# Attention into a token and channel mixer on one core: second token weights through SyncE's queue, token layer a pass later, first channel weights in two transfers

## The chip, the cores and the metric

The kernel runs on one core of one Trainium2 chip. The metric is the device time of one execution in microseconds; before, the median of three runs is 382.45 us (380.16 to 384.23). The engines are TensorE (PE, its weight loads PEld), VectorE (DVE), ScalarE (ACT), GpSimd (POOL) and SyncE (SP). SP here does nothing but issue DMA transfers; POOL issues DMA transfers too, and a transfer that changes the type (FP32 in memory, FP16 on chip) is issued by POOL in this kernel.

## The reference

```python
# q, k, v: (8, 12, 448, 64); tau = 0.1
q_n = q / (norm(q) + 1e-6);  k_n = k / (norm(k) + 1e-6)
attn = softmax(q_n @ k_n.T / tau)
x = (attn @ v) -> (8, 448, 768)                # heads side by side
h = relu(x.T @ w_tok1) @ w_tok2                # token mixer: 448 -> 256 -> 448
u = x + h.T
out = u + relu(u @ w_ch1) @ w_ch2              # channel mixer: 768 -> 1536 -> 768
```

Inputs and output are FP32; on chip the products are in FP16 with FP32 sums.

## The kernel before

**Pairs and passes.** Two heads of one batch make a pair; 6 pairs (`NPAIR`) make a batch, 48 pairs the whole. The order of every engine's work is written out by hand (`tc.manual_schedule()`): a prologue for pair 0, then a loop whose pass `i` handles pair `i`. Passes 1 to 5 are one loop, pass 6 is written out on its own, and from pass 7 on a third loop runs. Names with a number in this document (q10, v8, tok2(0)) mean the pair.

**What a pass does.** Loads run ahead: `load_qk(i + 6)` and `load_v(i + 4)`, each a 224 KB transfer (for the first twelve pairs) on SyncE's queue. `square(i + 3)` squares k on POOL and, in passes 1 to 5, q on ACT; `sums(i + 2)` adds them up on DVE; `norms` makes the reciprocal norms on ACT and DVE; `scaled(i + 1)` scales k and q into FP16 on POOL; `tpose(i + 1)` transposes them on PE. `score(i, c)` for four chunks c is a PE product followed by an exponential on ACT (L350). `cast_v` makes v FP16 on POOL. `pv_wide(i - 1)` and `x_wide(i - 1)` give the attention output x of the pair before.

**The token mixer.** `tok1(i)` multiplies x(i) by the first token weights and takes the relu on DVE. `tok2(i)` multiplies by `w2t`, the second token weights in their chunk order, and adds x on DVE, which gives u (L441). In passes 2 to 5 `tok1(i - 2)` and `tok2(i - 2)` are done in the same pass.

**From tokens to channels.** The channel mixer needs u transposed (`ut`). For the first two pairs of batch 0 `udma` does it with a DMA transpose on SyncE's queue (L447), issued at the ends of passes 2 and 3. Pairs 2 and 5 are transposed on PE and copied by ACT (`upose_act`), pairs 3 and 4 on PE and copied by DVE (`upose`). From pass 7 on a queue of channel products (`m_ch1`: L471, `m_ch2`: L487) is drawn from between the attention products. The first of them, six matmuls over the six parts of `ut`, stands in pass 7; its first matmul reads what udma(0) wrote, its second what udma(1) wrote.

**The weights.** POOL's queue loads them all, with the change of type: the first token weights in eight small transfers (`weights_tok1`), `w2n` (`weights_tok2`, 224 KB, early in the prologue), the first channel weights `wc1t` in four transfers of 576 KB (L203; a half of the columns and a half of the rows each), issued in passes 2, 4, 5 and 6, and later the second channel weights `wc2t` in two of 1152 KB (L208). `place_w2` (L198, pass 2) copies `w2n` into `w2t` on POOL with the columns taken in steps of four. `w2n` borrows one of the three buffers of the output rows (`ost`), which are first needed much later.

**Queues.** SyncE issues in the program's order, and an issue waits where its buffer is not free yet or where the eighth transfer before it has not landed. POOL issues its transfers between its own computations, in the program's order. Both queues are served by the same 16 DMA engines.

Of the kernel before, what the change touches and what calls it, by code (L numbers as in the profile page):

```python
# [7 lines left out]
FP32 = mybir.dt.float32  # L8
FP16 = mybir.dt.float16
# [13 lines left out]
def kernel(  # L23
# [12 lines left out]
    nc = tc.nc  # L36

    B, H, S, E = q.shape
    D = H * E
    T = moe_w_tok1.shape[1]  # L40
    C = moe_w_ch1.shape[1]
    SC = 112
    NCH = S // SC
    DT = D // 128
    CT = C // 128
    TT = T // 128
# [23 lines left out]
    def windows(b):  # L70
        return EVEN if b % 2 == 0 else ODD

    def pieces(lo, hi):
        got = []
        while lo < hi:
            c = lo // SC
            end = min(hi, SC * (c + 1))
            got.append((c, lo - SC * c, end - SC * c))
            lo = end
        return got  # L80
# [4 lines left out]
    outp = ctx.enter_context(tc.tile_pool(name="outp", bufs=3))  # L85
# [13 lines left out]
    def old(i):  # L99
        return i < OLD  # L100
# [12 lines left out]
    def load_rows(i, nm, src, bufs):  # L113
        h0 = 2 * (i % NPAIR)
        if old(i):
            t = pool_of(nm).tile([SC, QS, E], FP32, name=f"{nm}f_{i}", tag=f"{nm}f", bufs=bufs)
            nc.sync.dma_start(
                out=t[:].rearrange("p (g c) e -> p g (c e)", g=2),
                in_=src[h0:h0 + 2].rearrange("g (p c) e -> p g (c e)", c=NCH))
            return t  # L120
        t = pool_of(nm).tile([128, 2 * KC, E], FP32, name=f"{nm}f_{i}", tag=f"{nm}f", bufs=bufs)
        nc.sync.dma_start(out=t[:].rearrange("p (g c) e -> p g (c e)", g=2),
                          in_=src[h0:h0 + 2, 0:128 * KC].rearrange("g (p c) e -> p g (c e)", c=KC))
        return t

    def load_rest(i, nm, src):
        h0 = 2 * (i % NPAIR)
        t = (att if nm == "v" else rest).tile([128, HP, E], FP32, name=f"{nm}r_{i}", tag=f"{nm}r", bufs=4)
        for g in range(2):
            nc.sync.dma_start(out=t[64 * g:64 * g + 64],  # L130
                              in_=src[h0 + g:h0 + 2 * HP:2, 128 * KC:S].rearrange("j p e -> p j e"))
        return t
# [13 lines left out]
    def load_v(i):  # L146
        pipe[i]["v"] = load_rows(i, "v", v[i // NPAIR], 4)
        if not old(i) and "vr" not in half[i // HP]:
            half[i // HP]["vr"] = load_rest(i, "v", v[i // NPAIR])
# [7 lines left out]
    nc.gpsimd.memset(tiny[:], 1e-18)  # L157

    w1t = cst.tile([128, 5, T], FP16, name="w1t")
    w2n = outp.tile([128, TT, S], FP16, name="w2n", tag="ost")  # L160
    w2t = cst.tile([128, TT, S + 64], FP16, name="w2t")
    wc1t = cst.tile([128, DT, C], FP16, name="wc1t")
    wc2t = cst.tile([128, CT, D], FP16, name="wc2t")
# [17 lines left out]
    def weights_tok1(n0, n1):  # L181
        todo = []
        for m, (lo, hi) in enumerate(MAIN):
            r = 0
            for c, p0, p1 in pieces(lo, hi):
                todo.append((p1 - p0, m, r, c, p0))
                r += p1 - p0
        (c, p0, p1), = pieces(384, S)
        todo = sorted(todo + [(64, 3, 0, c, p0)]) + [(64, 4, 64, c, p0)]
        for n, m, r, c, p0 in todo[n0:n1]:  # L190
            nc.gpsimd.dma_start(out=w1t[r:r + n, m, :],
                                in_=moe_w_tok1.rearrange("(p c) t -> c p t", c=NCH)[c, p0:p0 + n])

    def weights_tok2():
        nc.gpsimd.dma_start(out=w2n[:], in_=moe_w_tok2.rearrange("(tt p) s -> p tt s", p=128))

    def place_w2():
        nc.gpsimd.tensor_copy(out=w2t[:, :, 0:S].rearrange("p t (c s) -> p t c s", c=NCH),  # L198
                              in_=w2n[:].rearrange("p t (s c) -> p t c s", c=NCH))

    def weights_ch1(i):
        cols, t = slice(768 * (i // 2), 768 * (i // 2) + 768), 3 * (i % 2)
        nc.gpsimd.dma_start(out=wc1t[:, t:t + 3, cols],  # L203
                            in_=moe_w_ch1[128 * t:128 * t + 384, cols].rearrange("(t p) c -> p t c", p=128))

    def weights_ch2(i):
        cols = slice(DH * i, DH * (i + 1))
# [48 lines left out]
    def some(i, a0, a1):  # L256
        sl, np_ = lay(i)
        return max(np_[a0:a1]), slice(sl[a0].start, sl[a1 - 1].stop)
# [9 lines left out]
    def norms(i, a0=0, a1=2, dve=False, rec=None):  # L268
        rec = dve if rec is None else rec
        st = pipe[i]  # L270
        n, sl = some(i, a0, a1)
        rn = st["rn"][0:n, sl]
        ne = nes[i % 3][0:n, sl]
        if dve:
            nc.vector.tensor_reduce(out=rn, in_=ne, axis=AXX.X, op=ALU.add)
            if not rec:
                return
        if dve or rec:
            nc.vector.reciprocal(out=rn, in_=rn)  # L279
            return  # L280
        nc.scalar.activation(out=rn, in_=st["ssq"][0:n, sl], func=AF.Ln, bias=tiny[0:n])
        nc.scalar.activation(out=ne[:, :, 0], in_=rn, func=AF.Exp, scale=0.5)
# [30 lines left out]
    def scaled(i):  # L313
        scale(i, 0)
        scale(i, 1)
# [102 lines left out]
    def tok1(i, wide=False):  # L418
        st = pipe[i]
        w1 = (0, 1, 2, 3) if (i // NPAIR) % 2 == 0 else (4, 0, 1, 2)  # L420
        psR = (ps2 if wide else ps).tile([128, TT, 128], FP32, name=f"psR_{i}", tag="s" if wide else "b")
        for tt in range(TT):
            for m in range(4):
                nc.tensor.matmul(psR[:, tt], w1t[:, w1[m], tt * 128:(tt + 1) * 128], st["x"][:, m],  # L424
                                 start=(m == 0), stop=(m == 3))
        st["rt"] = nrm.tile([128, TT, 128], FP16, name=f"rt_{i}", tag="rt", bufs=2)
        nc.vector.tensor_scalar_max(out=st["rt"][:], in0=psR[:], scalar1=0.0)  # L427

    def tok2(i, pe=False, wide=False):
        st = pipe[i]  # L430
        b, pj = i // NPAIR, i % NPAIR
        if pj == 0:
            u16[b] = mix.tile([128, DT, 4, 128], FP16, name=f"u16_{b}", tag="u16", bufs=4)
            ut[b] = mix.tile([128, DT, 4, 128], FP16, name=f"ut_{b}", tag="ut")
        psU = (ps2 if wide else ps).tile([128, 4, 128], FP32, name=f"psU_{i}", tag="s" if wide else "b")
        for m, lo in enumerate(windows(b)):
            for tt in range(TT):
                nc.tensor.matmul(psU[:, m], w2t[:, tt, lo:lo + 128], st["rt"][:, tt],  # L438
                                 start=(tt == 0), stop=(tt == TT - 1))
        u = u16[b][:, pj]  # L440
        nc.vector.tensor_tensor(out=u, in0=psU[:], in1=st["x"][:], op=ALU.add)  # L441
        if not pe:
            udma(i)

    def udma(i):
        b, pj = i // NPAIR, i % NPAIR
        nc.sync.dma_start_transpose(out=ut[b][:, pj], in_=u16[b][:, pj].rearrange("p m d -> p (m d)"))  # L447
# [28 lines left out]
    ost = {}  # L476
# [299 lines left out]
    with tc.manual_schedule():  # L776
# [3 lines left out]
            name=nc.get_next_instruction_name(), act_func_set_id=ACT_SET_LN_EXP,  # L780
# [7 lines left out]
        load_v(2)  # L788
        load_qk(5)
        load_v(3)  # L790
        weights_tok1(0, 7)

        square(0, 1, act=True)
# [7 lines left out]
        norms(0, 0, 1, dve=True)  # L801
        scale_part(0, 0, 0, 2, nc.gpsimd)
        scale_part(0, 0, 2, NCH, nc.gpsimd)
        weights_tok2()
        square(1, 1, act=True)
        square(1, 0, act=True)
        square(2, 1, act=True)
# [35 lines left out]
        for i in range(1, NPAIR):  # L843
            if i == 1:
                scale(2, 0)
                scale(2, 1, nc.vector)
            else:
                scaled(i + 1)
                if i == 3:
                    weights_tok1(7, 8)  # L850
                else:
                    weights_ch1(max(i - 3, 0))
            load_qk(i + 6)
            score(i, 0)
            score(i, 1)
            sums(i + 2)
            norms(i + 2)
            if i >= 2:
                tok1(i - 2)
            pv_wide(i - 1)  # L860
            x_wide(i - 1)
            norms(i + 2, dve=True)
            cast_v(i)
            if i == 2:
                place_w2()
            square(i + 3, 0)
            if i == 1:
                warm(10)
            score(i, 2)
            score(i, 3)  # L870
            tpose(i + 1)
            if i >= 2:
                tok2(i - 2, pe=True)
            square(i + 3, 1, act=True)
            load_v(i + 4)
            if 2 <= i < 4:
                udma(i - 2)

        i = NPAIR
        load_qk(i + 6)  # L880
# [2 lines left out]
        score(i, 1)  # L883
        sums(i + 2)
        norms(i + 2)
        tok1(i - 2)
        pv_wide(i - 1)
        x_wide(i - 1)
# [7 lines left out]
        upose_act(i - 4, True)  # L896
        norms(i + 2, dve=True)
        scaled(i + 2)
        weights_ch1(3)
        tok1(i - 1)  # L900


# [216 lines left out]
```

## Time and profile before

| | us |
|---|---|
| median of three runs | 382.45 (380.16, 382.45, 384.23) |
| profiled execution | 381.04 |
| its span | 379.3 |
| PE busy in the span | 364.9 (96%) |
| POOL, DVE, ACT busy | 286.4, 246.3, 233.7 |
| PE idle in the first 10 us; from 10 to 40; from 40 to 340 | 3.6; 4.9; 0.5 |
| DMA moved | 64.35 MB, 170 GB/s over the span |

The profile's page counts an engine as busy while an instruction of it runs. PE's matmuls overlap, so its busy time is no measure of its rate, but a gap in it is a real gap. The rows that the next section shows are of four kinds: a table of stretches, the orders of time of single engines (start, duration, engine and line, what it writes and reads, and in brackets the idle time before it with what ended that), and, for one transfer, its issue (start) with the time from there to its landing.

### The profile page before, as it was taken

Reading aid. Unit: us, or ns where it says so; the run is one execution under the profiler, and the core shown is the slowest. Engines: PE = TensorE matmul, PEld = TensorE weight load, DVE = VectorE, ACT = ScalarE, POOL = GpSimd, SP = SyncE. Lnnn points to the kernel's source line nnn. Section 1 sums busy time; section 2 is a strip of 40 time slices with the busy share of each in tenths; the row PEclk is TensorE's granted clock in tenths of the full one; section 3 lists DMA queues with packets and bytes.
Section 4 is the critical chain, followed back from the end, with each engine's and each line's share of the span. In section 5 each row is a group of like instructions: output and inputs, shape, how many; then the busy total and the mean of one; then the engine's idle time right before and its main releaser. Section 6 shows DMA issues by size and latency. Waiting matters only on the chain.

```text
span 379.3 us, 10291 instructions
## 1 busy us (share of the span) xinstructions
PE 364.9 (96%) x4096; PEld 238.8 (63%) x4096; DVE 246.3 (65%) x560; ACT 233.7 (62%) x401; POOL 286.4 (76%) x414
## 2 busy tenths in 40 slices
PE   6789999999999999999999999999999999999994
PEld 5466666676657666667666666666666676655562
DVE  7788866776436674557544675466545776887963
ACT  5999887855665447855675466774677574526410
POOL 8899998978667577668657757767869987389760
PEclk9999999999999999999999999999999999999998
DMA  7999999989985888869895877997995874200144
GB/s 203 270 250 218 261 252 233 178 161 167 228 193 133 207 193 203 177 168 171 208 208 125 175 184 190 201 169 186 212 178 116 159 160 99 57 0 3 54 125 114
DMA packets 116256, 64.35 MB, mean 170 GB/s; under 512 B 72304, under 2 KB 112880, under 8 KB 116208
## 3 DMA queue, kind: packets, MB, share of 16 engines
q1 hardware_dynamic: 110208, 58.20, 69.0%
q0 software_dynamic: 5616, 5.21, 8.7%
q8 instruction: 32, 0.52, 0.6%
q10 hardware_dynamic: 384, 0.29, 0.2%
q14 instruction: 16, 0.13, 0.1%
HBM read 43.45 MB, written 11.01 MB: 144 GB/s over the span
## 4 chain that ended last, share of the span: by engine, by line
PE 84%; DMA 5%; DVE 4%; ACT 3%; POOL 2%; issue 0%; SPq 0%; DVEq 0%; POOLq 0%
PE psG L471 21%; PE psF L487 21%; PE psO L388 9%; PE psS L349 8%; PE psU L438 5%; PE psR L424 5%; DMA kf<-in_k_dram 4%; PE psY L591 3%; PE psYo L679 2%; ACT pt L350 2%; PE psX L591 2%; PE psQ L356 2%; PE psZ L591 1%; PE psO L371 1%; DMA qk<-kq 1%; PE psZo L679 1%
## 5 line engine op out<-in xcount | busy, mean ns | idle before, releaser
L350 ACT ACTIVATE pt<-psS 128x896 f16<-128x896 f32 (+1 forms) x156 | 132.7, 915 | 52.4 <-PE psS L349 52.4
L487 PE MATMUL psF<-wc2t,gt 128*128 128x384 f16 x504 | 88.4, 326 | 0.0
L471 PE MATMUL psG<-ut,wc1t 128*128 128x448 f16 x432 | 88.1, 352 | 0.0
L302 POOL TENSOR_TENSOR kq<-kf,rn 128x384 f16<-128x384 f32 (+1 forms) x47 | 41.8, 889 | 59.7 <-DVE rn L279 56.7
L487 PEld LDWEIGHTS <-gt 128*128 128x128 f16 x504 | 47.1, 98 | 27.8
L471 PEld LDWEIGHTS <-wc1t 128*128 128x128 f16 x432 | 40.2, 98 | 32.4
L474 ACT ACTIVATE gt<-psG 128x448 f16<-128x448 f32 x72 | 38.8, 539 | 33.2 <-PE psG L471 33.2
L266 DVE TENSOR_REDUCE ssq<-sq 128x15 f32<-128x960 f32 (+2 forms) x51 | 56.1, 1100 | 2.9 <-POOL kq L302 1.1
L427 DVE TENSOR_SCALAR rt<-psR 128x256 f16<-128x256 f32 x48 | 20.1, 418 | 50.8 <-PE psR L424 50.8
L302 POOL TENSOR_TENSOR kq<-qf,rn 112x512 f16<-112x512 f32 x45 | 46.9, 1043 | 3.0
L349 PE MATMUL psS<-qk 64*128 64x448 f16 x312 | 40.9, 353 | 3.5 <-DVE qk L328 2.6
L491 DVE TENSOR_TENSOR ost<-psF,u 128x384 f32<-128x384 f32 (+1 forms) x48 | 25.8, 537 | 26.8 <-PE psF L487 26.7
L250 POOL TENSOR_TENSOR sq<-kf 128x384 f32<-128x384 f32 (+1 forms) x46 | 40.1, 872 | 0.9 <-DMA kf<-in_k_dram 0.9
L250 POOL TENSOR_TENSOR sq<-qf 112x512 f32<-112x512 f32 x39 | 40.5, 1038 | 0.0
L388 PE MATMUL psO<-vt,pt 128*128 128x65 f16 (+1 forms) x1024 | 39.1, 193 | 0.0
L392 DVE TENSOR_TENSOR x<-psO,rec 128x256 f16<-128x256 f32 x82 | 34.8, 425 | 2.8
L388 PEld LDWEIGHTS <-pt 128*128 128x128 f16 (+1 forms) x1024 | 34.2, 97 | 3.5 <-issue 0.9
L441 DVE TENSOR_TENSOR u<-psU,x 128x512 f16<-128x512 f32 x48 | 32.4, 674 | 2.3 <-PE psU L438 0.9
L438 PE MATMUL psU<-rt,w2t 128*128 128x128 f16 x384 | 29.3, 219 | 0.9 <-POOL w2t L198 0.9
L438 PEld LDWEIGHTS <-w2t 128*128 128x128 f16 x384 | 24.8, 98 | 8.4 <-POOL w2t L198 1.1
L424 PEld LDWEIGHTS <-w1t 128*128 128x128 f16 x384 | 24.8, 98 | 7.9 <-issue 2.1
L424 PE MATMUL psR<-x,w1t 128*128 128x128 f16 x384 | 29.3, 219 | 0.2 <-DVE u L441 0.2
(128 smaller groups left out, 478.4 us busy)
## 6 DMA issues: line engine op xcount, KB each, us to landing
qf<-in_q_dram SPq DMA_DIRECT2D x47, 224.0 KB, 4.0
kf<-in_k_dram SPq DMA_DIRECT2D x36, 192.0 KB, 3.6
vf<-in_v_dram SPq DMA_DIRECT2D x36, 192.0 KB, 3.6
vf<-in_v_dram SPq DMA_DIRECT2D x12, 224.0 KB, 8.3
kf<-in_k_dram SPq DMA_DIRECT2D x11, 224.0 KB, 8.2
wc1t<-in_moe_w_ch_dram POOLq DMA_DIRECT2D x4, 576.0 KB, 10.0
wc2t<-in_moe_w_ch_dram POOLq DMA_DIRECT2D x2, 1152.0 KB, 12.2
out_dram<-ost SPq DMA_DIRECT2D x6, 336.0 KB, 4.4
```

The lines of the kernel that those rows point to most:

```text
L250: nc.gpsimd.tensor_mul(out=dst, in0=src, in1=src)
L266: nc.vector.tensor_reduce(out=st["ssq"][0:n, sl], in_=st["sq"][0:n, sl], axis=AXX.X, op=ALU.add)
L302: eng.tensor_tensor(out=kq[0:p, a, 0:n].rearrange("p c g e -> p g c e"), in0=st["kq"[a]][:].rearrange("p (g c) e -> p g c e", g=2), in1=_b ...
L349: nc.tensor.matmul(psS[:, hh, 0:S], qk[hb, c * n:c * n + 128], qm[hb], start=True, stop=True)
L350: nc.scalar.activation(out=pts[i % 2][0:n, 2 * S * c:2 * S * (c + 1)].rearrange("p (h s) -> p h s", h=2), in_=psS[0:n, :, 0:S], func=AF.Ex ...
L388: nc.tensor.matmul(psO[:, m, 0:E + 1], pts[i % 2][0:n, at:at + 128], vt[0:n, i % HP, nch * hh + c, 0:E + 1], start=(old(i) and c == 0), st ...
L392: nc.vector.tensor_tensor(out=st["x"][:, :, hh * E:(hh + 1) * E], in0=psO[:, :, 0:E], in1=_bcast_free(rec[:], E), op=ALU.mult)
L424: nc.tensor.matmul(psR[:, tt], w1t[:, w1[m], tt * 128:(tt + 1) * 128], st["x"][:, m], start=(m == 0), stop=(m == 3))
L438: nc.tensor.matmul(psU[:, m], w2t[:, tt, lo:lo + 128], st["rt"][:, tt], start=(tt == 0), stop=(tt == TT - 1))
L471: nc.tensor.matmul(psG[:, 0:S], wc1t[:, dt, ct * 128:(ct + 1) * 128], ut[b][:, dt].rearrange("p m s -> p (m s)")[:, lo:lo + S], start=(dt ...
L474: nc.scalar.activation(out=gt[:, ct, (b % 2) * S:(b % 2 + 1) * S], in_=psG[:, 0:S], func=AF.Relu)
L487: nc.tensor.matmul(psF[:, 0:hi - lo], gt[:, ct, at:at + 128], wc2t[:, ct, lo:hi], start=(ct == 0), stop=(ct == CT - 1))
```

## The change

1. `w2n` becomes two FP32 tiles of 128 x 768, of which 448 columns are used, in two of the three `ost` buffers. They are loaded by SyncE, one 224 KB transfer each, behind `load_v(3)` and so ahead of v4, q6, k6 and all later loads. POOL no longer issues a transfer for them.
2. `place_w2` becomes two POOL copies that also change the type, in pass 3 instead of pass 2.
3. `tok2` comes a pass later: tok2(0) in pass 3, tok2(1) in pass 4, tok2(2) in pass 5; pass 6 has tok2(3), at a place of its own ahead of `tok1(4)`, and tok2(4) where it was. From pass 7 on nothing is moved.
4. The two `udma` follow: udma(0) at the end of pass 3, udma(1) at the end of pass 4. In SyncE's queue udma(1) now stands behind q10, k10 and v8.
5. `wc1t` is loaded in two transfers of 1152 KB (all rows, a half of the columns), issued in passes 2 and 4, instead of four in passes 2, 4, 5 and 6.

```diff
-    w2n = outp.tile([128, TT, S], FP16, name="w2n", tag="ost")
+    w2n = [outp.tile([128, D], FP32, name=f"w2n{tt}", tag="ost") for tt in range(TT)]
...
     def weights_tok2():
-        nc.gpsimd.dma_start(out=w2n[:], in_=moe_w_tok2.rearrange("(tt p) s -> p tt s", p=128))
+        for tt in range(TT):
+            nc.sync.dma_start(out=w2n[tt][:, 0:S], in_=moe_w_tok2[128 * tt:128 * tt + 128, :])
 
     def place_w2():
-        nc.gpsimd.tensor_copy(out=w2t[:, :, 0:S].rearrange("p t (c s) -> p t c s", c=NCH),
-                              in_=w2n[:].rearrange("p t (s c) -> p t c s", c=NCH))
+        for tt in range(TT):
+            nc.gpsimd.tensor_copy(out=w2t[:, tt, 0:S].rearrange("p (c s) -> p c s", c=NCH),
+                                  in_=w2n[tt][:, 0:S].rearrange("p (s c) -> p c s", c=NCH))
 
     def weights_ch1(i):
-        cols, t = slice(768 * (i // 2), 768 * (i // 2) + 768), 3 * (i % 2)
-        nc.gpsimd.dma_start(out=wc1t[:, t:t + 3, cols],
-                            in_=moe_w_ch1[128 * t:128 * t + 384, cols].rearrange("(t p) c -> p t c", p=128))
+        cols = slice(C // 2 * i, C // 2 * i + C // 2)
+        nc.gpsimd.dma_start(out=wc1t[:, :, cols], in_=moe_w_ch1[:, cols].rearrange("(t p) c -> p t c", p=128))
...
         load_v(3)
+        weights_tok2()
         weights_tok1(0, 7)
...
-        weights_tok2()
...
                 if i == 3:
                     weights_tok1(7, 8)
-                else:
-                    weights_ch1(max(i - 3, 0))
+                elif i < 5:
+                    weights_ch1((i - 2) // 2)
...
-            if i == 2:
+            if i == 3:
                 place_w2()
...
-            if i >= 2:
-                tok2(i - 2, pe=True)
+            if i >= 3:
+                tok2(i - 3, pe=True)
...
-            if 2 <= i < 4:
-                udma(i - 2)
+            if 3 <= i < 5:
+                udma(i - 3)
...
         norms(i + 2)
+        tok2(i - 3, pe=True)
         tok1(i - 2)
...
-        weights_ch1(3)
```

## The prediction

> **What bounds the kernel now.** I read the table of stretches first, to see where TensorE has no slack. Its columns are the stretch, its length, then each engine's busy time (instructions in brackets), the granted clock, the DMA share and GB/s.
>
> ```profile
> 10.00:40.00 30.00, 25.15 (x422) 18.09 (x422) 26.16 (x58) 29.19 (x49) 28.74 (x33) 1.00 1.16 246
> 40.00:60.00 20.00, 19.93 (x258) 12.83 (x256) 13.84 (x31) 15.71 (x27) 18.68 (x23) 1.00 1.18 251
> 60.00:80.00 20.00, 20.00 (x257) 13.35 (x254) 13.69 (x33) 13.53 (x24) 17.59 (x31) 1.00 1.07 186
> ```
>
> Until 40 us PE (first figure) has idle time, while ACT (fourth) works 29.19 of 30 us and POOL 28.74. From 40 us on PE is full. Whatever delays PE there reaches the end one for one; whatever is saved before 40 counts only as far as PE enters pass 7 sooner. The DMA engines are full throughout (share above 1).
>
> Next the PE and ACT orders of time around the change:
>
> ```profile
> 22.10 0.62 PE L438 MATMUL psU<-rt,w2t 128*128 128x128 f16 x8 [0.90 <-POOL w2t L198]
> ...
> 42.54 1.30 PE L471 MATMUL psG<-ut,wc1t 128*128 128x448 f16 x6
> ```
>
> ```profile
> 23.05 1.72 ACT L350 ACTIVATE pt<-psS 112x896 f16<-112x896 f32 x2 [0.20 <-PE psS L349]
> ```
>
> The first line is the wait that the change can remove: tok2(0) sat 0.90 us behind `place_w2`. But of it only 0.20 us reached ACT, the engine that sets the pace there. The second line is the first channel product of pass 7, six matmuls, the second of which reads what udma(1) writes.
>
> Then the issues with their time to landing, read as start plus the last figure: the two middle wc1t transfers, udma(1), and four loads of SyncE's queue (v3, v4, v8, q11; the number is the pair).
>
> ```profile
> L203 POOL DMA_DIRECT2D wc1t<-in_moe_w_ch_dram x1: 803/803/803, 29.1 to 29.1; - x1
> ...
> DMA to landing us min/median/max: 10.6/10.6/10.6
> ...
> L203 POOL DMA_DIRECT2D wc1t<-in_moe_w_ch_dram x1: 804/804/804, 33.5 to 33.5; - x1
> ...
> DMA to landing us min/median/max: 10.5/10.5/10.5
> ...
> L447 SPq DMA_TRANSPOSE ut<-u x1: 1499/1499/1499, 27.6 to 27.6; - x1
> ...
> DMA to landing us min/median/max: 6.6/6.6/6.6
> ...
> L117 SPq DMA_DIRECT2D vf<-in_v_dram x1: 313/313/313, 11.5 to 11.5; - x1
> ...
> DMA to landing us min/median/max: 9.5/9.5/9.5
> ...
> L117 SPq DMA_DIRECT2D vf<-in_v_dram x1: 313/313/313, 13.1 to 13.1; - x1
> ...
> DMA to landing us min/median/max: 8.7/8.7/8.7
> ...
> L117 SPq DMA_DIRECT2D vf<-in_v_dram x1: 313/313/313, 30.6 to 30.6; - x1
> ...
> DMA to landing us min/median/max: 11.1/11.1/11.1
> ...
> L140 SPq DMA_DIRECT2D qf<-in_q_dram x1: 495/495/495, 31.0 to 31.0; - x1
> ...
> DMA to landing us min/median/max: 13.2/13.2/13.2
> ```
>
> Landings: wc1t 39.7 and 44.0, so one 576 KB transfer drains in 4.3 us. udma(1) 34.2, which is 8.3 us before PE wants it at 42.5. v3 21.0 and v4 21.8: alone, SyncE's queue delivers a 224 KB load per 0.85 us. v8 41.7 and q11 44.2: while a wc1t transfer drains, one per 2.5 us. So each 576 KB of wc1t throws SyncE's queue back by 4.3 x (1 - 0.85/2.5) = 2.8 us. That price decides the case.
>
> **Part by part, POOL and the first 40 us.** Removed from POOL: the w2n issue (0.81 us at 8.46) and two wc1t issues (0.80 each). The two that stay carry 1152 KB; the nearest row is the 1152 KB wc2t issue, 1.07 us (the lower bound 0.80, that of 576 KB). `place_w2` was one copy of 0.98 us; two of 448 columns from FP32 cost 0.98 together at least, and at most two casts of 512 columns (0.62 each), 1.24. I take 1.1, nearer the casts, whose types it has. The w2n saving is worth nothing: POOL then waited 0.47 for k2 and 0.74 for a norm anyway. Pass 2 loses 0.98 and gains 0.28, so square(5,0) starts at 21.3, not 22.0. Pass 3 adds 1.1: `place_w2` ends near 26.5, tok2(0) on PE starts then, where tok2(1) had started at 25.6, and scores of pair 4 are queued behind it; ACT's exponentials of pair 4 (27.24) come about 0.3 late. The wait has moved a pass, not gone. Pass 4 issues the second transfer (+0.28), so square(7,0) ends 0.28 + 1.1 + 0.28 - 0.98 = 0.7 later, and DVE's sums(7), then ACT's norms(7), which had 0.16 of slack, come up to 0.5 late. Pass 6 holds two tok2: eight more matmuls (0.61 on PE, which has idle time there) and one more u addition (0.61 to 0.69) on DVE, behind which x(5) and tok1(5) wait. Against this stand up to 0.45 from k4, for which POOL waited at 16.7 while w2n was draining beside it, and the issues missing in passes 5 and 6. Altogether PE reaches pass 7 between 0.4 sooner and 1.0 later. I set this at nothing, because the next part covers it; without that cover it counts in full.
>
> **SyncE's queue and udma(1).** The program gives SyncE's transfers eight semaphores in turn, and each issue waits for the one eight before; they land in order. Before, udma(1) stood ahead of q10, k10 and v8. Now it stands behind them, and its landing is, from 34.2:
>
> - two w2n loads ahead of it: +2 x 0.85 = +1.7;
> - the w2n transfer of POOL's queue no longer beside it: -2.8 x 224/576 = -1.1;
> - the first wc1t transfer 576 KB longer: +2.8;
> - q10, k10, v8 ahead of it: +2.6;
> - the second transfer, 1152 KB, issued near 29.5 as before and drained to about 43, now falls ahead of it: +2 x 2.8 = +5.7;
> - udma(0), moved into that drain: a transpose at 51.8, in the drain of wc2t, landed 4.3 us after the transfer ahead of it, against 0.7 alone (30.2 to 30.9). It takes 4.3 of the drain's 8.6 us from the loads, 1.7 loads or 1.5 us, less its own 0.7: +0.8 (bounds 0 and +1.5);
> - pauses in the queue that can be filled: 227 GB/s from 22 to 34 us against 264 from 16 to 22, so 12 x 37/264 = 1.7 us at most. I take -0.5, since an issue must still wait for the eighth before it.
>
> 34.2 + 1.7 - 1.1 + 2.8 + 2.6 + 5.7 + 0.8 - 0.5 = 46.2. The second matmul of the first channel product ran at 42.54 + 0.19 = 42.7 and now waits until 46.2: +3.5 us, PE standing with the whole order behind it. Since PE is full afterwards, it stays to the end. What is late next: k10 near 44.6, which POOL's square(10,0) wanted at 43.8; that hides under the stall. The second half of the first channel weights lands near 45 and is first read about 57, so it costs nothing. On the range: with all pauses filled and no price for udma(0), 44.2 (+1.5); with none and 1.5, 47.4 (+4.7).
>
> The profiled execution took 381.04 (span 379.3 and 1.74 around it), 1.41 under the median 382.45 of three runs (380.16 to 384.23). So 381.04 + 3.5 = 384.5 for it, and 382.45 + 3.5 = 385.9 for the median.
>
> A rule of the Trainium skill speaks for the change here. "DMA: Bandwidth & Descriptors", section "Bandwidth", advises batching to at least 1 MiB; its fit gives about 2.0 us fixed for each transfer. By that two transfers fewer would save an estimated 4 us and udma(1) would land near 42.2, in time. The trace shows two queued 576 KB transfers landing 4.3 us apart with SyncE's queue held to a third all the while: bytes, no fixed part to save. I go by the rows.
>
> **The rivals.**
> 1. The transpose itself is caught in the drain. If wc1t still drains when udma(1)'s turn comes, it costs 4.3 instead of 0.7. For it: the drain ends near 43 and could slip to 46. Against: three loads stand ahead, which alone take the queue past 43. Adding 1 to 3.6 us: about 388, up to 389.5.
> 2. udma(1) lands by 42.7 and the moved `place_w2` decides: +0.4 to +1.0, 383.2. For it: POOL full from 17 to 50 us. It needs 3.5 us less on the queue than my sum.
> 3. Not slower: POOL's relief. It decides only if udma(1) lands by 42.7; then k4 (0.45), ACT's 0.20 and up to 1.04 of net issue time bring pass 7 forward: 382.45 - 1.7 = 380.8. Against it: ACT has 0.8 us of idle time in 30, and it is not POOL alone that paces.
>
> **How the numbers follow.** Forecast 0.56, rival 1 0.26, rival 2 0.09, rival 3 0.09. A measurement here tells about 1% (3.8 us) from no change. The forecast lies close under that bound, so half of it, 0.28, is beyond: slower 0.28 + 0.26 = 0.54. Within: 0.28 + 0.09 + 0.04 = 0.41; faster, the far end of rival 3, 0.05. The forecast's own range is 384.0 to 387.2; the one given reaches to rival 1 and, below, to no change: 382.3 to 389.8.
>
> **What would show it.** Right: TensorE idle 3 to 4 us inside the first L471 group, ended by the ut transfer, with udma(1) landing near 46; wc1t landing in two, near 33 and 43 to 45; v8 landing after 43; `place_w2` at about 25.4, and PE still waiting for it in pass 3; PE full from there. Wrong: udma(1) landing before 42.7, or no idle time at L471, or PE gaps after 50 us that were not there before.

## The result and the profile after

| | before | after |
|---|---|---|
| median, us (6 runs each) | 381.00 (380.16 to 384.23) | 392.97 (390.43 to 396.95) |
| profiled execution, us | 381.04 | 393.71 |
| its span, us | 379.3 | 391.9 |
| ratio, 95% interval | | 1.0281 (1.0227 to 1.0335) |

The changed kernel is slower by about 12 us, where the prediction had 3.5. The six runs before are the three of the first table and three more. The ratios, here and below, compare mean times and leave out a run that fell in the chip's slower state (396.95 here, 388.67 and 389.15 among the experiments), while medians and ranges hold every run. Line numbers after the change are one higher (L471 is now L472, L447 is L448). Where the time lies is seen first in the table of stretches of the changed kernel (columns as before: length, then PE, PEld, DVE, ACT and POOL busy, granted clock, DMA share, GB/s). The last line is of the kernel before.

```profile
40.00:60.00 20.00, 11.35 (x124) 6.95 (x122) 7.48 (x18) 7.93 (x13) 11.79 (x13) 0.74 1.05 196
60.00:80.00 20.00, 20.00 (x255) 12.74 (x254) 13.08 (x31) 15.71 (x27) 13.39 (x20) 1.00 1.04 189
...
36.00:44.00 8.00, 7.35 (x130) 5.71 (x126) 6.82 (x17) 7.56 (x12) 5.07 (x7) 1.00 0.98 87
44.00:54.00 10.00, 1.64 (x31) 1.03 (x28) 3.12 (x7) 2.09 (x5) 3.41 (x5) 0.70 1.20 167
...
36.00:44.00 8.00, 7.81 (x131) 5.79 (x128) 6.99 (x14) 6.97 (x11) 8.00 (x10) 1.00 1.13 263
```

PE worked 19.93 of the 20 us from 40 to 60 before and works 11.35 now; from 60 on it is full again, so what is lost there is never won back. From 36 to 44 us the DMA engines moved 87 GB/s, where they had moved 263. PE's waits (us in total, times, longest) and PE's order of time name the place:

```profile
PE psG L472 <- DMA ut<-u: 8.4, 2, 4.7
...
PE psU L439 <- POOL w2t L200: 1.2, 2, 0.7
```

```profile
26.87 0.56 PE L439 MATMUL psU<-rt,w2t 128*128 128x128 f16 x7 [0.69 <-POOL w2t L200]
...
41.50 0.61 PE L425 MATMUL psR<-x,w1t 128*128 128x128 f16 x8 [0.19 <-DVE u L442]
...
48.85 0.53 PE L472 MATMUL psG<-ut,wc1t 128*128 128x448 f16 x1 [3.74 <-DMA ut<-u]
54.06 2.02 PE L472 MATMUL psG<-ut,wc1t 128*128 128x448 f16 x5 [4.68 <-DMA ut<-u]
56.02 0.56 PE L350 MATMUL psS<-qk 64*128 64x448 f16 x2
```

The rows of the kernel before that these are set against:

```profile
39.09 0.61 PE L424 MATMUL psR<-x,w1t 128*128 128x128 f16 x8 [0.16 <-DVE u L441]
...
43.77 0.36 PE L349 MATMUL psS<-qk 64*128 64x448 f16 x2
```

It is the first channel product of pass 7, as predicted, but both of its first two matmuls wait: the first for udma(0), 3.74 us, the second for udma(1), 4.68. The score behind it started at 43.77 before and starts at 56.02, 12.25 later. This is made up of 2.4 us of later entry (tok1(5) at 41.50, 39.09 before), 8.4 of waits, 1.25 by which the six matmuls themselves are longer (0.53 and 2.02 against 1.30 for all; the granted clock was 0.50 from 47.9 to 58.2), and 0.2 between.

The issues of the two `udma` and of the second wc1t transfer, with their time to landing:

```profile
L448 SPq DMA_TRANSPOSE ut<-u x1: 1309/1309/1309, 29.4 to 29.4; - x1
...
DMA to landing us min/median/max: 19.3/19.3/19.3
...
L448 SPq DMA_TRANSPOSE ut<-u x1: 7709/7709/7709, 38.6 to 38.6; - x1
...
DMA to landing us min/median/max: 15.4/15.4/15.4
...
L205 POOL DMA_DIRECT2D wc1t<-in_moe_w_ch_dram x1: 912/912/912, 29.8 to 29.8; - x1
...
DMA to landing us min/median/max: 22.7/22.7/22.7
```

udma(0) lands at 48.7, udma(1) at 54.0 and not at 46.2; the issue of udma(1) alone holds SyncE for 7.7 us (1.5 before). The weights land at 52.5, not near 44. So everything on both queues is late, and not only the transposes. The DMA view shows it directly. Its GB/s line cuts the stretch that was asked for into 40 slices. For the changed kernel from 34 to 54 us (0.5 us each):

```profile
GB/s 275 238 247 198 164 190 113 97 73 49 42 46 43 46 47 38 42 90 169 144 156 137 167 155 252 240 258 250 251 215 213 168 116 91 63 59 62 44 223 229
```

From 38.5 to 42.5 the rate lies between 38 and 49 GB/s, and from 51 to 53 between 44 and 63. It isn't for want of transfers: the second weight transfer was under way until 52.5, k9 landed at 41.5 and k10 at 52.7, and POOL stood 2.44 and 6.59 us for these two. And for the kernel before, from 26 to 36 us (0.25 us each):

```profile
GB/s 287 240 242 287 307 320 296 283 267 197 166 108 79 29 25 28 275 269 215 281 314 279 289 320 307 300 292 316 19 57 339 197 289 225 211 219 252 244 223 262
```

Here too the rate falls to 25 and to 19 GB/s, from 29.0 to 30.0 and from 33.0 to 33.5: short holes that end just before the two transposes land, at 30.9 and 34.2. They were there to be read before the change. The prediction averaged over them (227 GB/s from 22 to 34 us) and called them pauses that could be filled.

What stands still in a hole is told by the single packets, the pieces in which the trace records a transfer. In the changed kernel a packet of 256 bytes from SyncE's queue (the transposes') took 0.018 us at the median and one of 1536 bytes from POOL's queue (the weights') 0.134. But 6 and 13 of them, begun between 35.1 and 38.6 us, all ended between 42.8 and 43.1, the longest after 7.84 us; and 16 more of SyncE's queue, begun between 48.4 and 51.2, all ended between 53.1 and 53.3.

### The profile page after: what moved, and what is told of

Read it like the earlier page. It is cut to its first block, busy times and chain, and to the rows that moved or that the text cites. A ratio compares the mean times of both kernels' runs of the same rounds, so it can differ in the third digit from the quotient of the medians.

```text
span 391.9 us, 10290 instructions
## 1 busy us (share of the span) xinstructions
PE 370.6 (95%) x4096; PEld 242.2 (62%) x4096; DVE 246.2 (63%) x560; ACT 234.6 (60%) x401; POOL 285.8 (73%) x412
## 4 chain that ended last, share of the span: by engine, by line
PE 85%; DMA 6%; ACT 3%; DVE 3%; POOL 1%; issue 0%; DVEq 0%; ACTq 0%; POOLq 0%
PE psG L472 21%; PE psF L488 20%; PE psO L389 9%; PE psS L350 8%; PE psU L439 5%; PE psR L425 5%; DMA ut<-u 4%; PE psY L592 3%; ACT pt L351 3%; PE psYo L680 2%; PE psX L592 2%; PE psQ L357 2%; PE psZ L592 1%; PE psO L372 1%; PE psZo L680 1%; DMA qk<-kq 1%
## 5 line engine op out<-in xcount | busy, mean ns | idle before, releaser
L472 PE MATMUL psG<-ut,wc1t 128*128 128x448 f16 x432 | 89.8, 356 | 8.4 <-DMA ut<-u 8.4
L472 PEld LDWEIGHTS <-wc1t 128*128 128x128 f16 x432 | 40.5, 99 | 42.0 <-issue 10.1
L350 PE MATMUL psS<-qk 64*128 64x448 f16 x312 | 41.5, 359 | 3.6 <-DVE qk L329 3.1
L389 PEld LDWEIGHTS <-pt 128*128 128x128 f16 (+1 forms) x1024 | 34.2, 97 | 3.6 <-PE psS L350 1.0
```

The lines of the kernel that those rows point to most:

```text
L350: nc.tensor.matmul(psS[:, hh, 0:S], qk[hb, c * n:c * n + 128], qm[hb], start=True, stop=True)
L389: nc.tensor.matmul(psO[:, m, 0:E + 1], pts[i % 2][0:n, at:at + 128], vt[0:n, i % HP, nch * hh + c, 0:E + 1], start=(old(i) and c == 0), st ...
L472: nc.tensor.matmul(psG[:, 0:S], wc1t[:, dt, ct * 128:(ct + 1) * 128], ut[b][:, dt].rearrange("p m s -> p (m s)")[:, lo:lo + S], start=(dt ...
```

## The experiments

Two theories were set against each other. By the *pace* theory, that of the prediction, the transposes are late because the queue's bytes are shared with the weights. By the *barrier* theory a DMA transpose that meets a long drain (a weight transfer still being worked off) holds nearly all traffic of the core until it is through. Two more were tried on the way: that a halved PE clock costs time, and that the parts of the change cost something each by themselves.

**Parts alone: four transfers again.** The changed kernel with the wc1t transfers as before.

```diff
-                elif i < 5:
-                    weights_ch1((i - 2) // 2)
+                else:
+                    weights_ch1(max(i - 3, 0))
...
+        weights_ch1(3)
```

> The changed kernel with the first channel weights back in four 576 KB transfers (passes 2, 4, 5, 6); everything else of the change stays. Barrier theory (a DMA transpose issued while a weight transfer drains holds packets on most DMA engines until the slowest engine has reached it): udma(0) now reaches the engines near the end of the first, shorter drain, but udma(1) still stands in the drain of the second and third transfers, so it lands at 45 to 50 us and TensorE still waits for it at the first channel product, 3 to 7 us; 384 to 388 us. Rival (pace alone, as in the prediction: 2.8 us per 576 KB): udma(1) lands near 43.4, at most 1 us of wait, 381.5 to 383 us.

Measured 382.67 against 381.55, ratio 1.0034 (0.9997 to 1.0070). The `udma` landed at 33.8 and 44.2. The rate from 36 to 44 was still only 132 GB/s:

```profile
36.00:44.00 8.00, 7.59 (x141) 6.21 (x140) 6.45 (x15) 7.26 (x12) 7.87 (x10) 1.00 1.31 132
```

The time was below what was expected and inside the pace theory's range; the hole in the rate was the barrier theory's, though these transfers have 576 KB. Both are so because udma(1) came only 1.5 us after the 42.7 at which PE wants it: most of the hole went into the 8.3 us of slack that the kernel before had there. (The rows are of an execution of 385.10, one of the three slowest of ten.)

**Parts alone: two transfers only.** The kernel before, with the two 1152 KB transfers and nothing else.

```diff
-                else:
-                    weights_ch1(max(i - 3, 0))
+                elif i < 5:
+                    weights_ch1((i - 2) // 2)
...
-        weights_ch1(3)
```

> The kernel before with the two 1152 KB transfers in passes 2 and 4 as its only change. udma(0) and udma(1) are then both in or just behind the first drain (22 to 33 us). Barrier theory: a stretch of some microseconds around 28 to 34 us in which the DMA engines move little, udma(1) landing near 36 to 40, still before TensorE reads it at 42.5: 380 to 383 us. Rival (pace): udma(1) at 34.2 + 2.8 = 37, no slow stretch, 380 to 382 us. Both say that the size of the transfers alone does not make the loss; a time over 386 us would say that it does.

Measured 387.03 against 381.55, ratio 1.0129 (1.0066 to 1.0192): more than either theory gave. Its stretch and the next row that suffered, on POOL:

```profile
36.00:44.00 8.00, 7.81 (x132) 5.83 (x129) 6.85 (x14) 7.02 (x11) 6.32 (x8) 1.00 0.93 121
```

```profile
48.53 1.04 POOL L249 TENSOR_TENSOR sq<-kf 112x512 f32<-112x512 f32 x1 [5.80 <-DMA kf<-in_k_dram]
```

udma(1) was issued at 27.2 and landed at 42.5, just in time for PE. But the hole (121 GB/s) put off the loads behind it: k10 landed at 48.4, POOL stood 5.80 us, and PE then 2.66 for x. So the size of the transfers alone costs 1.3%, by the same hole, through another wait.

**Parts alone: the later pass.** The kernel before with only `place_w2`, `tok2` and `udma` a pass later.

```diff
-            if i == 2:
+            if i == 3:
                 place_w2()
...
-            if 2 <= i < 4:
-                udma(i - 2)
+            if 3 <= i < 5:
+                udma(i - 3)
```

> The kernel before with only the order moved: place_w2, tok2 and the two udma a pass later; second token weights through POOL's queue as before, first channel weights in four transfers. Barrier theory: udma(1) comes to lie in the drain of the second and third transfers (34 to 42 us) and lands at 44 to 50, TensorE waits 2 to 7 us at the first channel product: 383 to 388 us. Rival (pace): 34.2 + 2.6 + 2.8 x 1 to 1.5 = 40 to 41, no wait, 380.5 to 382 us.

Measured 381.52 against 381.55, ratio 1.0012 (0.9990 to 1.0034): nothing in the median, which is the pace theory's time and not the barrier theory's, though in the profiled execution, its slowest run of ten with 384.4, udma(1) landed at 44.7 and PE waited 1.75. Size alone 1.3%, order alone nothing, all but the size 0.3%, together 2.8%: the parts don't add up, they meet. The load of `w2n` through SyncE's queue was not tried alone.

**The transposes off the DMA.** The changed kernel with pairs 0 and 1 transposed on PE and copied by DVE in pass 5.

```diff
-            if 3 <= i < 5:
-                udma(i - 3)
+            if i == 5:
+                upose(0, 2)
```

> The changed kernel with pairs 0 and 1 transposed on TensorE in pass 5 (eight more transposes there, one more VectorE copy of 0.69 us), so no DMA transpose before 50 us; the loads and both 1152 KB transfers stay. Barrier theory: the stretch from 35 to 53 us runs at 230 GB/s or more instead of 77 to 200, the second weight transfer lands near 43 to 45 us instead of 52.5, k10 before 46, no DMA wait at the first channel product; what stays is the later entry into pass 7 (2.4 us) and little more: 382.5 to 385 us. Rival (the weights and SyncE's loads are slow in each other's company, transposes or not): the second transfer still lands after 50, POOL still waits 2 to 6 us for k9 and k10, 387 us or more.

Measured 383.34 against 381.55, ratio 1.0043 (1.0013 to 1.0072).

```profile
36.00:44.00 8.00, 7.42 (x127) 5.74 (x125) 7.09 (x15) 7.26 (x12) 5.88 (x7) 1.00 1.13 254
44.00:54.00 10.00, 9.93 (x133) 6.40 (x130) 7.98 (x18) 8.05 (x15) 8.93 (x10) 1.00 1.12 234
```

The hole is gone (254 GB/s where it was 87), the second weight transfer lands at 44.2, as the prediction's pace had it, and PE has no wait for `ut`. What is left is the later entry: tok1(5) at 41.71 in this execution (384.49).

**The same bytes, not transposed.** This tells the bytes of the two transfers from their being transposes. Plain copies of the same 128 KB at the same places of the same queue; the transposition of two pairs is left out.

```diff
             if 3 <= i < 5:
-                udma(i - 3)
+                nc.sync.dma_start(out=ut[0][:, i - 3], in_=u16[0][:, i - 3])
```

> The changed kernel with the two DMA transposes of pairs 0 and 1 replaced by plain DMA copies of the same 128 KB at the same places in SyncE's queue, so these two pairs enter the channel mixer untransposed; waits, order, bytes and weight transfers are the changed kernel's. Barrier theory: no packets held, the stretch from 35 to 44 us runs at 230 GB/s or more, the second weight transfer lands near 44 to 45 instead of 52.5, the copy for pair 1 near 47 to 48 (it still stands behind q10, k10 and v8), so TensorE waits some 2 to 4 us instead of 8.4: 385 to 387 us. Rival (the place in the queue and the weight drain alone make the loss): the copies land near 48 and 53 as the transposes did, 390 us or more.

Measured 383.69 against 380.69, ratio 1.0074 (1.0047 to 1.0102). The DMA view from 34 to 54 us, the stretch, and PE at the first channel product:

```profile
GB/s 248 232 230 278 216 223 239 226 233 244 240 242 233 237 245 252 314 306 292 256 260 240 222 209 204 216 241 240 282 222 191 285 255 281 227 207 252 249 179 158
```

```profile
36.00:44.00 8.00, 7.32 (x138) 5.94 (x136) 6.97 (x15) 7.28 (x11) 6.65 (x9) 1.00 1.13 250
```

```profile
45.01 1.11 PE L472 MATMUL psG<-ut,wc1t 128*128 128x448 f16 x5 [1.53 <-DMA ut<-u]
```

Same bytes, same queue, same place: no slice under 158 GB/s. The second copy lands at 45.0, the second weight transfer at 45.4, and the time is 3.0 us over the kernel before and below the 385 to 387 expected. This is near the pace that the prediction worked out. No packet between 24 and 54 us took over 1.3 us. Some 8 us of the 12 by the ratios (2.8% less 0.7%), 9 by the medians, go with the transposing, not with the bytes or with the place in the queue.

**The same bytes in small pieces.** A transpose might be dear because it is cut small. The same copies in 512 pieces of 254 bytes each, near the transposes' 512 of 256; they leave out the last column of each block, which is set to zero, and the transposition as above.

```diff
+            if i == 3:
+                nc.vector.memset(ut[0][:, 0:2, :, 127], 0.0)
             if 3 <= i < 5:
-                udma(i - 3)
+                nc.sync.dma_start(out=ut[0][:, i - 3, :, 0:127], in_=u16[0][:, i - 3, :, 0:127])
```

> As e5 (plain copies in place of the two DMA transposes), but each copy is cut into 512 pieces of 254 bytes, near the 512 pieces of 256 bytes that a transpose moves; column 127 of each block is set to zero beforehand, so these two pairs enter untransposed and cut. Barrier theory (it is the transpose that holds packets): the copies land within 2 us of those of e5 (40.3 and 45.0), the stretch from 36 to 44 us stays above 200 GB/s, 383 to 386 us. Rival (many small pieces beside a weight transfer are slow, transposed or not): landings at 46 and 50 or later, under 150 GB/s from 36 to 44, 388 us or more.

Measured 386.52 (four runs: 383.00, 384.76, 388.29, 389.15) against 381.05, ratio 1.0117 (1.0052 to 1.0183). The copies landed at 42.3 and 46.0, the rate from 36 to 44 was 237 GB/s, PE waited 1.03. So there is no hole by small pieces either. These rows are of the run of 384.76, which they explain; why two of the four runs lie 3.5 and 4.4 us higher stays open.

**The second transfer moved away.** The changed kernel with the second 1152 KB transfer at the end of pass 6, behind both transposes.

```diff
-                elif i < 5:
-                    weights_ch1((i - 2) // 2)
+                elif i == 2:
+                    weights_ch1(0)
...
+        weights_ch1(1)
```

> The changed kernel with the second 1152 KB transfer issued at the end of pass 6, where the kernel before had its fourth, instead of in pass 4; nothing else. Barrier theory: both transposes then fall in the gap between the two drains, udma(0) lands near 36 and udma(1) near 40, no DMA wait at the first channel product; the second half of the weights lands near 55, before it is read; what stays is the later entry into pass 7: 382.5 to 384.5 us. Rival (udma(1) behind q10, k10, v8 is late in any case): udma(1) after 44.9 and a wait of 2 us or more, 385 us or more.

Measured 381.49 against 380.69, ratio 1.0030 (1.0013 to 1.0047). The rate from 34 to 54 us, and udma(1):

```profile
GB/s 276 201 97 31 79 145 277 307 309 321 203 23 20 241 250 326 328 361 328 327 312 209 350 311 309 253 204 223 212 241 245 227 240 241 242 235 253 233 224 264
```

```profile
L448 SPq DMA_TRANSPOSE ut<-u x1: 1787/1787/1787, 34.6 to 34.6; - x1
...
DMA to landing us min/median/max: 6.8/6.8/6.8
```

Each transpose still makes its hole (31 GB/s at 35.5, 20 at 40), but only 1 to 1.5 us long, much as before the change; udma(1) lands at 41.4, in time. The time is a microsecond below what was expected. What remains, 0.8 us, is entry into pass 7: the product starts at 43.78, 1.24 later than before.

**The large transfers without DMA transposes.** The kernel before, two 1152 KB transfers, pairs 0 and 1 transposed on PE.

```diff
-            if 2 <= i < 4:
-                udma(i - 2)
+            if i == 4:
+                upose(0, 2)
```

> The kernel before with two 1152 KB first channel transfers (as e2) and pairs 0 and 1 transposed on TensorE in pass 4, so the large transfers stay and the DMA transposes are gone. Barrier theory: no stretch under 200 GB/s between 22 and 50 us, k10 lands before 45, POOL waits at most 1 us for it: 381 to 382.8 us. Rival (1152 KB in one transfer is the harm, transposes or not): k10 near 48 again, POOL waiting 5 us for it, 385 us or more.

Measured 380.24 against 380.69, ratio 0.9994 (0.9970 to 1.0017), with 248 GB/s from 36 to 44. The large transfers do no harm where no DMA transpose meets them, and give nothing that can be measured. A gain of theirs that the PE transposes take back, or the other way about, isn't excluded. It was the best candidate for a version that beats both kernels, and only ties with the one before.

**Is it the clock? At the entry.** The transposes on PE as above, and 24 matmuls on the identity ahead of tok2(0), so that PE doesn't stand there.

```diff
+            if i == 3:
+                warm(24)
             if i >= 3:
                 tok2(i - 3, pe=True)
```

> e3 with 24 idle matmuls on TensorE ahead of tok2(0) in pass 3, where TensorE waited 0.50 and 0.69 us for place_w2 and the granted clock was then 0.5 for 3.4 us. If the half clock makes a part of the later entry into pass 7: granted clock 1.00 from 26 to 31 us, tok1(5) ahead of pass 7 at about 40.5 instead of 41.7, 382.0 to 382.8 us, ratio to before near 1.002. Rival (the half clock costs nothing, ACT would have waited anyway for place_w2): tok1(5) still near 41.7, ratio 1.004 as e3.

Measured 383.44 against 380.69, ratio 1.0065 (1.0045 to 1.0085). The granted clock was 1.00 from 20 to 36 us, tok1(5) still at 41.06. The clock theory missed; nothing is won.

**Is it the clock? At the stall.** The changed kernel with 120 such matmuls ahead of the first channel product, and the changed kernel again beside it.

```diff
             fed[0] += fed[1]
+            if i == NPAIR + 1:
+                warm(120)
             unit(True)
```

> The changed kernel with 120 idle matmuls (about 6.7 us of TensorE) ahead of the first channel product in pass 7, where TensorE stood from 45 to 54 us and the granted clock was 0.5 until 58.1. Clock theory: the wait for the transposes stays, the granted clock is 1.00 after it, the five matmuls behind it take 1.1 us instead of 2.0, and the time is 1.5 to 2.5 us under that of e11 in the same comparison. Rival (the half clock hides in time that is lost anyway): within 0.7 us of e11.

> The changed kernel itself once more, to stand beside e9 and e10 on one chip. Both theories: 390 to 394 us, two waits for transposes at the first channel product, 7 to 9 us together, and a granted clock of 0.5 after them.

Measured 392.57, ratio 1.0342 (1.0270 to 1.0414), and 391.98, ratio 1.0295 (1.0263 to 1.0326). The first of them, in the stretches and in PE's order of time, and the second, in PE's order of time:

```profile
54.00:60.00 6.00, 6.00 (x82) 3.90 (x80) 2.39 (x5) 3.40 (x5) 6.00 (x8) 1.00 1.12 298
```

```profile
43.66 3.51 PE L341 MATMUL warm<-id 128*128 128x128 f16 x60
49.50 5.15 PE L341 MATMUL warm<-id 128*128 128x128 f16 x60 [2.32 <-issue]
54.48 1.30 PE L472 MATMUL psG<-ut,wc1t 128*128 128x448 f16 x6
```

```profile
46.83 0.39 PE L462 MATMUL psT<-id,u 128*128 128x128 f16 x2 [6.85 <-issue]
47.02 1.06 PE L425 MATMUL psR<-x,w1t 128*128 128x128 f16 x8
...
54.37 1.11 PE L472 MATMUL psG<-ut,wc1t 128*128 128x448 f16 x5 [1.65 <-DMA ut<-u]
```

With the extra matmuls the time is 0.6 us longer, where the clock theory wanted 1.5 to 2.5 us less. But this tests the clock less well than it was meant to. The repeat had no half clock behind its stall either (1.00 from 51.4 on, five matmuls in 1.11 us), and the 120 matmuls, held up by 2.32 us of "issue" and by a granted clock of 0.50 from 49.7 to 53.1, filled PE until udma(1) landed, so that no wait was left to see. What the half clock cost is read from the first profile of the changed kernel alone: the 1.25 us in the sum above, in an execution that took 393.71, against 392.17 and 392.24 for these two.

The repeat is of more use than it was made for: where two waits for `ut` of 7 to 9 us in all were expected, PE stood 6.85 us by "issue" *ahead* of pass 7, with tok1(5) at 47.02, then 1.65 for `ut`, and yet the second matmul ran at 54.37. In the three profiles of the changed order udma(1) was issued at 38.6, 43.3 and 34.7 and landed at 54.0, 54.55 and 54.3, and the three medians lie within 1 us, whatever PE did before. The landing of udma(1) sets the end, to within the microsecond or so that the clock can add.

**All together.** The time for which the rate was under 125 GB/s between 24 and 54 us, counted in slices of 0.25 us of the profiled execution, for each kernel:

| kernel | DMA transposes | wc1t transfers | under 125 GB/s, us | udma(1) landed | ratio |
|---|---|---|---|---|---|
| changed | 2, later | 2 | 9.25 | 54.0 | 1.028 |
| changed, again | 2, later | 2 | 8.5 | 54.3 | 1.030 |
| changed, 120 matmuls more | 2, later | 2 | 8.75 | 54.55 | 1.034 |
| before, two transfers | 2 | 2 | 7.25 | 42.5 | 1.013 |
| changed, four transfers | 2, later | 4 | 5.0 | 44.2 | 1.003 |
| before, a pass later | 2, later | 4 | 4.5 | 44.7 | 1.001 |
| changed, second transfer late | 2, later | 2 | 2.5 | 41.4 | 1.003 |
| before | 2 | 4 | 1.75 | 34.2 | 1 |
| plain copies; pieces; PE (twice) | none | 2 | 0 | 45.0; 46.0; none | 1.007; 1.012; 1.004 and 0.999 |
| PE, 24 matmuls more | none | 2 | 0.25 | none | 1.006 |

## Why the prediction was right or wrong

**Right: the place, the path and the sign.** PE stands inside the first channel product for what `udma` writes, because the transposes now lie behind q10, k10 and v8 and in the drain of the second large transfer; PE is full from there (20.00 of 20 us), so the delay stays to the end. The last step of the sum holds in size as well: the delay is the landing of udma(1) less 42.7. 381.0 + 54.0 - 42.7 = 392.3, measured 392.97; for the plain copies 380.69 + 45.0 - 42.7 = 383.0, measured 383.69. With the plain copies the loss is 3.0 us, close to the 3.5 that the sum gave.

**Right: the pace, as a whole.** For a transfer without transposing the queue delivered about what the sum said: 45.0 (plain copies) and 46.0 (pieces), against 46.2. Its single terms (1.7, 1.1, 2.8, 2.6, 5.7) were not measured apart, so errors among them may have cancelled. The first wc1t transfer landed at 33.8 (predicted near 33), the second, without transposes, at 44.2 and 45.4 (43 to 45).

**Wrong: "udma(0), moved into that drain ... +0.8 (bounds 0 and +1.5)".** This is the step that failed: the price of a transpose in the drain, for udma(0), and with it for udma(1), to which the sum gave no price beyond its old one. It is what parts 46.2 from 54.0, 7.8 us. The step took a transpose in a drain for one more transfer that takes its share. The runs showed that it holds the rest: 87 GB/s from 36 to 44 us against 250 with plain copies. One hole of 5.75 us stands ahead of udma(0), one of 3.25 ahead of udma(1); no run priced the two apart. The price came from one row, the transpose at 51.8 in the drain of wc2t, which landed 4.3 us after the transfer ahead of it. In the trace of before no slice from 50 to 62 us falls under 191 GB/s: that transpose makes no hole, and so was the wrong one to take. The two in the first 40 us did make holes, and were nearer. The "0.7 alone (30.2 to 30.9)" could not show this: it is the difference of two landings, and udma(0)'s hole, from 28.75 to 30.0, ended before both.

**Wrong in kind: "pauses in the queue that can be filled ... -0.5".** The pauses were these holes. They are no room for other transfers, and were longer beside the large ones. An average over 12 us hid them, and so did the DMA share from which the engines were called "full throughout"; slices of 0.25 us show them.

**Rival 1 was the true one in kind, and too small.** "The transpose itself is caught in the drain" is what happened, but priced at 4.3 per transpose from the same row it reached only 389.5. "Three loads stand ahead, which alone take the queue past 43" counted against it, as though the drain would end on its own time; the transposes lengthen it, from 44 to 52.5.

**Wrong, but covered: pass 7's entry, "between 0.4 sooner and 1.0 later".** `place_w2` took 1.91 us, two casts of 0.99 each, not 1.1, though it started at 24.90 as foreseen (near 25.4); tok2(0) still waited 0.51 and 0.69 for it. tok1(5) came 0.6 (plain copies) to 2.6 us (transposes on PE) later than before, in the changed kernel 2.4; why these differ so was not followed up. As said, the wait for udma(1) covered this: with the second transfer away it is what is left, 0.8 us.

**Right, as far as shown: no fixed cost to save.** The rule of the Trainium skill that the prediction weighed ("DMA: Bandwidth & Descriptors", section "Bandwidth", with the fixed 2.0 us of its section "Anatomy of one DMA — SWDGE (gpsimd) path") would have saved an estimated 4 us by the larger transfers. They gave 0.9994 (0.9970 to 1.0017) where no DMA transpose met them, in a kernel that also transposes two pairs on PE, and cost 1.3% where the transposes did.

A second page bears on the step that failed. "Advanced Engine Details and Errata", section "X-Bar Transpose (TRN2)", says that TRN2 transpose DMAs are as fast as regular ones. Over the whole of the changed kernel nothing speaks against it: the 42 transposes onto `ut`, of 128 KB, landed 3.3 us after their issue at the median, the 224 KB loads of q 4.0. Beside the second 1152 KB transfer it doesn't hold: 19.3 and 15.4 us, where plain copies in their places took 12.5 and 11.0 and cost the kernel 8 to 9 us less. The measurement decides.

**Open.** What makes the hole long. That a transpose must gather all 16 DMA engines, which a large transfer beside it sets apart, is argued, not shown. It fits the holes: 0.5 to 1.25 us for each transpose in the kernel before, some 3 to 6 beside the second 1152 KB transfer, but also 2.5 to 4.5 where the transfers have 576 KB and udma(1) falls among two of them, and none for copies. It fits the landings too, each recorded as 16 signals: those of the second weight transfer came over 9.9 us (42.6 to 52.5) in the changed kernel and over 3.5 with plain copies, those of udma(1) within 0.2 us, those of the plain copy over 3.3. Why the transpose at 51.8 makes no hole; the same one in the kernel with the second transfer late, issued at 52.3 beside wc2t, made one of over 2 us (57.5 to 59.75, down to 11 GB/s). Whether the 6.85 us of "issue" in the repeat is PE's instruction supply held up in the same hole. And why the two kernels with copies scatter by 6 us in their runs.

## What to carry to other kernels

Before moving a DMA transpose or making a weight load larger, cut the DMA view into slices shorter than a microsecond around the transposes there are: a hole in the rate ahead of a transpose's landing, while other transfers are under way, was the sign here that the transpose holds them, and an average over ten microseconds hid it. Keep transposes out of long drains: issue the large load behind them, or transpose on TensorE; either gave back some 10 to 11 of the 12 us here. Price a moved piece by the nearest row with the same neighbours, and try the parts of a change in company as well as alone: here the order cost nothing, the size 1.3%, and the whole change 2.8%.

## What the runs showed of the hardware that was not expected

- Two 128 KB DMA transposes beside a 1152 KB transfer brought the core's whole DMA rate down to 38 to 49 GB/s for 4 us and to 44 to 63 for 2, the loads of both queues included, and SyncE's issue of the second took 7.7 us. Beside copies of the same bytes at the same places it never fell under 158 GB/s in 0.5 us slices.
- In such a hole packets of both queues stood still together: 19 that began over 3.4 us, of 256 and 1536 bytes, ended within 0.3 us of each other, after up to 7.84 us. In the five kernels whose first DMA transpose is issued after 50 us, no packet begun from 24 to 50 took over 1.3.
- The granted clock was 0.50 for 10.2 us around PE's stall in one execution of the changed kernel, where six matmuls took 2.55 us instead of 1.30; in another execution it was back at 1.00 before udma(1) landed, and the total was 392.24 instead of 393.71.
- PE stood 6.85 us by "issue" in one execution of the changed kernel and not in another, and the one with it was not the longer (392.24 and 393.71).
- Two POOL copies from FP32 with a stride in the source took 0.99 us each for 448 columns, where one FP16 copy of both halves had taken 0.98 in all.
